# Seven products instead of eight for the last batch's first MLP product

## The chip, the cores and the metric

The kernel runs on one core of a Trainium2 chip. A core has five engines with their own instruction queues: TensorE (PE; matmuls, its weight loads are shown as PEld), VectorE (DVE), ScalarE (ACT), GpSimd (POOL) and SyncE (SP, which here only starts DMA transfers). Matmul results go to PSUM, which has eight banks of 512 floats in each of 128 partitions; everything else lives in SBUF. The metric is device time in microseconds of one execution, lower is better.

## The reference

There are 8 batches of 576 rows. First a linear attention over 8 heads of 64 columns, with position weights, then a low-rank mixing over the rows, then a two-layer MLP:

```python
r = np.maximum(x, 0.0)                         # x is q or k
phi = np.concatenate([r * cos, r * sin], -1)   # 128 features a head
kv = np.einsum('bhsf,bhsd->bhfd', k_p, v)
z = np.sum(k_p, axis=2)
x = np.einsum('bhsf,bhfd->bhsd', q_p, kv) / (np.einsum('bhsf,bhf->bhs', q_p, z) + 1e-6)
h = x.transpose(0, 2, 1) @ U @ V               # rank 32, over the rows
u = x + h.transpose(0, 2, 1)
out = u + np.maximum(u @ w_ch1, 0.0) @ w_ch2   # 512 -> 2048 -> 512
```

What matters here is `u @ w_ch1`, with relu, for one batch: 576 x 512 by 512 x 2048.

## The kernel before, in words

Of a batch's 576 rows, 512 are handled as four tiles of 128 rows ("main"), and the 64 rows left over ("tail") of two batches together make one more tile of 128. `uT[b]` holds the batch's u transposed: four blocks d of 128 channels, each with 4 x 128 rows. `w1_bf` and `w2_bf` hold the two weight matrices in 16 bits.

The work is laid out by hand as a list of slots. Each slot is one unit of matmuls; `todo` attaches other work (features, transposes, loads, sums) to slot numbers. Every engine takes its instructions in the order in which this list issues them; semaphores are set by the framework from what each instruction reads and writes. `starts[b]` is the slot at which batch b's first product begins. For each pair of batches there are, in this order: 16 slots of the even batch's first product, its 14 slots of the second product, 16 slots of the odd batch's first product, 4 slots of the pair's tail rows through the first layer, 14 slots of the odd batch's second product, 4 slots of the tail through the second layer.

The first product, `g1_main(b, j)`, makes 128 of the 2048 hidden columns in one slot: four matmuls (one for each channel block d) of 128 weights by 512 rows into one bank of the three called "g"; ScalarE applies the relu and writes 512 values to `hid[b]` (L550, L559). `g1_tail` does the same for the pair's tail rows, sixteen 128-column matmuls a slot, with one ScalarE relu (L570, L577).

The second product, `w_part(b, n)`, already uses a 2 x 2 block algorithm of the Strassen kind with seven products (Winograd's form): hidden columns are split into even and odd blocks of 128, rows into two halves of 256, and output columns into two halves. Seven steps of two slots each (`step, half = divmod(n, 2)`), 16 matmuls of 256 columns a step. The sums of weights, T, are made early in the kernel (`w2_form`); the sums of hidden blocks, S, are made by VectorE in halves (`hid_form(b, n, half)`, L696): form 1 is S1, form 2 is S2, form 3 is written over a block of `hid`, form 4 is S4. Half 0 covers the first four of the eight hidden blocks of a kind, half 1 the others; the first slot of a step reads half 0 alone. Results are joined by ScalarE (step 0's copy, `w_sum`), VectorE (L740) and GpSimd (three adds of `w_sum` and u, L740), and stored.

PSUM is used by tags: "g" has three banks, "T" one, "X" a pair of banks; two more are "oA" and "oB" in the beginning and, from slot 32 on (`pair_o`), one pair "O" for the attention's products. In SBUF, `qst`, `kst` and `vst` are the staging into which SP loads q, k and v of a batch, 10 KB a partition each. `k_p` and `q_p` hold the features made from them (8 KB each).

For the last batch, b = 7, the attention work is done when its first product begins; what runs beside it is only `hid_form` on VectorE.

Of the kernel before, what the change touches and what calls it, by code (L numbers as in the profile page):

```python
# [17 lines left out]
def kernel(  # L18
# [13 lines left out]
    B = 8  # L32
# [16 lines left out]
    def tail(b):  # L49
# [3 lines left out]
    const = ctx.enter_context(tc.tile_pool(name="const", bufs=1))  # L53
    pool = ctx.enter_context(tc.tile_pool(name="work", bufs=2))
    ps = ctx.enter_context(tc.tile_pool(name="ps", bufs=1, space=bass.MemoryType.PSUM))
    ps_rest = [ExitStack()]
    ps_o = ps_rest[0].enter_context(
        tc.tile_pool(name="ps_o", bufs=1, space=bass.MemoryType.PSUM)
    )

    ctx.enter_context(tc.manual_schedule())


    qst = const.tile([P, H, 5, D], FP32)
    kst = const.tile([P, H, 5, D], FP32)
    vst = const.tile([P, H, 5, D], FP32)

    def nines(src, b):
        return src[b].rearrange("h (m k) d -> m h (k d)", k=9)
# [40 lines left out]
    def cast(eng, o, i):  # L110
        if eng is nc.scalar:
            nc.scalar.activation(out=o, in_=i, func=AF.Copy, bias=0.0, scale=1.0)
        else:
            eng.tensor_copy(out=o, in_=i)  # L114
# [126 lines left out]
            G_.tensor_copy(out=V_qt[quarter(d), d, :], in_=V_tl[quarter(d), :])  # L241

    G3, T1, X1, OA, OB, O1 = ("g", 3), ("T", 1), ("X", 1), ("oA", 1), ("oB", 1), ("O", 1)
    turn = [0]

    def O2():
# [2 lines left out]

    def pair_o():  # L250
        ps_rest[0].close()
        ps_rest[0] = ctx.enter_context(
            tc.tile_pool(name="ps_O", bufs=1, space=bass.MemoryType.PSUM)
        )

    def bank(shape, dt, tag, bufs, name):
        if tag in ("oA", "oB"):
            return ps_o.tile(shape, dt, tag=tag, bufs=bufs, name=name)
        if tag == "O":
            t = ps_rest[0].tile([P, 2, 512], FP32, tag=tag, bufs=bufs, name=name)  # L260
            return t if len(shape) == 3 else t[:, 0, 0 : shape[1]]
        return ps.tile(shape, dt, tag=tag, bufs=bufs, name=name)

# [271 lines left out]

    hid, hid_tl = {}, {}

    g_open = {}

    def g1_main(b, j, half=False):  # L540
# [22 lines left out]
    def g1_tail(pr, jq):  # L563
        if pr not in hid_tl:
            hid_tl[pr] = pool.tile([P, NJ, P], BF16, tag="hid_tl", bufs=1, name="hid_tl")
        g_ps = ps.tile([P, 4, P], FP32, tag="g", bufs=3, name="gt_ps")
        for jj in range(4):
            j = jq * 4 + jj
            for d in range(4):
                nc.tensor.matmul(  # L570
                    out=g_ps[:, jj, :],
                    lhsT=w1_bf[:, d, j * P : j * P + P],
                    rhs=uT_tl[pr][:, d, :],
                    start=(d == 0),
                    stop=(d == 3),
                )
        nc.scalar.activation(  # L577
            out=hid_tl[pr][:, jq * 4 : jq * 4 + 4, :], in_=g_ps, func=AF.Relu,
            bias=0.0, scale=1.0,
        )  # L580
# [44 lines left out]
    def g2_tail(pr, part):  # L625
        last = pr == NPAIR - 1
        if part == 0 or last and part == 3:
            tag, bufs = T1 if part == 0 else O1
            o_ps[pr] = bank([P, DM], FP32, tag, bufs, "ot_ps")
        o = o_ps[pr]  # L630
        if last:
            cols = slice(0, 384) if part < 3 else slice(384, DM)
            js = (range(0, 5), range(5, 10), range(10, NJ), range(NJ))[part]
        else:
            cols, js = slice(0, DM), range(part * 4, part * 4 + 4)
        for j in js:
            nc.tensor.matmul(  # L637
                out=o[:, cols], lhsT=hid_tl[pr][:, j, :], rhs=w2_bf[:, j, cols],
                start=(j == 0), stop=(j == NJ - 1),
            )  # L640
        if js[-1] < NJ - 1:
            return
        if part == 2 or not last:
            o_sb[B + pr, 0] = pool.tile([P, DM], FP32, tag="o_tl", bufs=1, name="o_tl")
        o_s = o_sb[B + pr, 0]
        nc.vector.tensor_tensor(
            out=o_s[:, cols], in0=u_tl[pr][:, cols], in1=o[:, cols], op=ALU.add
        )
        for i in range(2):
            eng = store_eng(2 * pr) if part == 2 or not last else (nc.sync, nc.scalar)[i]  # L650
            eng.dma_start(
                out=out[2 * pr + i].rearrange("(m k) n -> m k n", k=9)[:, 4, cols],
                in_=o_s[i * TS : i * TS + TS, cols],
            )
# [21 lines left out]
    def hid_block(b, i, r, rows=slice(0, KB)):  # L676
        h = hid[b].rearrange("p (k i) t -> p k i t", i=2)
        return h[:, rows, i, r * 256 : r * 256 + 256]
# [30 lines left out]
    def w_part(b, n):  # L709
        step, half = divmod(n, 2)  # L710
        lhs, rhs, to = (
            (lambda: hid_block(b, 0, 0), w2_block(0, 0), 0),
            (lambda: s_forms[b, 2], T[1], 1),
            (lambda: s_forms[b, 1], T[0], 2),
            (lambda: s_forms[b, 3], T[2], 3),
            (lambda: hid_block(b, 1, 0), w2_block(1, 0), 0),
            (lambda: s_forms[b, 4], w2_block(1, 1), 2),
            (lambda: hid_block(b, 1, 1), T[3], 3),
        )[step]
        lhs = lhs()  # L720
        opens = step < 4
        if opens and half == 0:
            tag, bufs = T1 if to == 0 else G3
            w_ps[to] = bank([P, DM], FP32, tag, bufs, f"w_ps{to}")
        res = w_ps[to].rearrange("p (g n) -> p g n", g=2)
        for k_ in range(half * 4, half * 4 + 4):
            for g in range(2):
                nc.tensor.matmul(  # L728
                    out=res[:, g, :], lhsT=lhs[:, k_, g * P : g * P + P], rhs=rhs[:, k_, :],
                    start=(opens and k_ == 0 and g == 0),  # L730
                    stop=(k_ == KB - 1 and g == 1), skip_group_check=not opens,
                )
        for f in {0: (1, 2), 2: (3,), 4: (4,)}.get(n, ()):
            hid_form(b, f, 1)
        if half == 0:
            return
        lo, hi = slice(0, HD), slice(HD, DM)

        def add(eng, o, x, y):
            eng.tensor_tensor(out=o, in0=x, in1=y, op=ALU.add)  # L740

        def by_d(t):
            return t.rearrange("p c (d n) -> p d c n", n=P)

        def u(c0, h):
            return u_bf[b][:, 2 * h : 2 * h + 2, c0 : c0 + 2, :]

        if step == 0:
            w_sum[b] = pool.tile([P, 2, HD], FP32, tag="w_sum", bufs=1, name="w_sum")
            cast(A_, w_sum[b], res)  # L750
        elif step == 1:
            w = w_sum[b]
            o0, o1 = o_alloc(b, 0), o_alloc(b, 1)
            add(V_, w, w, res)
            add(G_, by_d(o1[:, :, hi]), by_d(w), u(2, 1))
            add(G_, by_d(o0[:, :, hi]), by_d(w), u(0, 1))
            add(G_, by_d(o1[:, :, lo]), by_d(w), u(2, 0))
        elif step == 2 or step == 3:
            o = o_sb[b, 1][:, :, hi]
            add(V_, o, o, res)  # L760
        elif step == 4:
            add(V_, by_d(o_sb[b, 0][:, :, lo]), u(0, 0), by_d(res))
        elif step == 5:
            o = o_sb[b, 0][:, :, hi]
            add(V_, o, o, res)
            store_w(b, 0, 0)
        else:
            o = o_sb[b, 1][:, :, lo]
            add(V_, o, o, res)
            store_w(b, 2, 1)  # L770
# [16 lines left out]
    def lay(units, in_second):  # L787
        slots.extend(units)
        second.extend([in_second] * len(units))

    def first_units(b):
        starts[b] = len(slots)
        lay([lambda j=j: g1_main(b, j) for j in range(NJ)], False)
        for i in range(4 * (b > 0)):
            beside.setdefault(starts[b] + (12 + 2 * i if b == 1 else 8 + i), []).append(
                lambda i=i: hid_form(b, (1, 2, 4, 3)[i], 0)
            )

    def second_units(b):
        lay([lambda n=n: w_part(b, n) for n in range(14)], True)  # L800
# [3 lines left out]
    def lay_all():  # L804
        for pr in range(NPAIR):
            e, o = 2 * pr, 2 * pr + 1
            first_units(e)
            if pr == 0:
                lay([lambda cc=cc, p=p: g2_part(cc, p) for p in range(4) for cc in range(4)], True)
            else:  # L810
                second_units(e)
            first_units(o)
            lay([lambda j=j, pr=pr: g1_tail(pr, j) for j in range(4)], False)
            second_units(o)
            lay([lambda p=p, pr=pr: g2_tail(pr, p) for p in range(4)], True)

# [239 lines left out]
    def gate(src):  # L1056
        nc.sync.dma_start(out=mark2, in_=src)
# [47 lines left out]
    def put(at, thunk):  # L1105
        todo.setdefault(at, []).append(thunk)

    put(15, lambda: gate(w2_bf[0:1, 4, 0:1]))
    put(70, release)
    put(72, release)  # L1110
    for n, t in enumerate(loads(2)):
# [38 lines left out]
```

## Time and profile before

| | us |
|---|---|
| median of 3 runs | 297.22 (296.43 to 297.79) |
| the profiled execution | 296.9 |
| its span, from the first to the last instruction | 295.1 |
| last batch: first matmul of the first product | 257.71 |
| first matmul of the tail rows | 271.52 |
| first matmul of the second product | 275.09 |
| first matmul of the tail's second layer | 287.32 |

The mean granted TensorE clock was 0.997. In a row of the timeline the first number is the start in us from the beginning of the span, the second the length of the group; matmuls are pipelined, so the time that one takes from the next is read from starts, not from the length of one. In a group's row the count stands behind x, then busy us and mean ns of one, then the idle time of its engine just before it and what ended that.

### The profile page before, as it was taken

The page shows a single profiled execution, that of the slowest core. Times are in us where ns is not written, and L with a number is a line of the kernel's source. Part 1 is how long each engine was busy: PE and PEld are TensorE (multiplying, and loading weights), DVE is VectorE, ACT ScalarE, POOL GpSimd, SP SyncE. Part 2 cuts the span into 40 slices and gives each one's busy share as a digit, 9 for nine tenths or more (in the row PEclk, how much of TensorE's full clock was granted, in tenths as well). Part 3 has the DMA queues.
Part 4 walks back from the last instruction along what each step waited for, and adds up shares of the span by engine and source line. Part 5 has one row for each costly group of instructions (what it writes and reads, how often), then busy time and mean ns, then how long its engine had stood idle before and what let it go on. Part 6 is the DMA issues. An engine that isn't in the chain of part 4 may idle for free.

```text
span 295.1 us, 7056 instructions
## 1 busy us (share of the span) xinstructions
PE 289.5 (98%) x2946; PEld 194.9 (66%) x2946; DVE 182.7 (62%) x358; ACT 159.1 (54%) x273; POOL 72.2 (24%) x113
## 2 busy tenths in 40 slices
PE   8999999999999999999999999999999999999994
PEld 6876455445987547855887547855887547845982
DVE  4979648897884578537744587537744586404331
ACT  2955641675692557646692557746692453066300
POOL 8430600140062304540051500540051101400040
PEclk9999999999999999999999999999999999999998
DMA  6999999999999995999679708995374104030004
GB/s 200 355 254 252 274 205 263 262 183 173 280 202 190 300 343 126 257 291 296 146 128 244 292 2 203 209 318 147 73 133 169 38 2 89 2 142 2 1 2 178
DMA packets 85283, 53.30 MB, mean 181 GB/s; under 512 B 54020, under 2 KB 82980, under 8 KB 85252
## 3 DMA queue, kind: packets, MB, share of 16 engines
q1 hardware_dynamic: 78804, 41.40, 58.1%
q0 software_dynamic: 6368, 11.43, 16.1%
q8 instruction: 23, 0.38, 0.5%
q14 instruction: 8, 0.07, 0.1%
q10 hardware_dynamic: 80, 0.03, 0.0%
HBM read 36.86 MB, written 9.44 MB: 157 GB/s over the span
## 4 chain that ended last, share of the span: by engine, by line
PE 98%; DVE 0%; ACT 0%; issue 0%
PE g_ps L550 38%; PE w_ps L728 29%; PE gt_ps L570 5%; PE o_ps L610 5%; PE ot_ps L637 5%; PE w_ps L200 3%; PE x_ps L412 3%; PE kv_ps L338 2%; PE a_ps L438 1%; PE va_ps L463 1%; PE kv_ps L319 1%; PE t_ps L355 1%; PE t_ps L367 1%; PE xh_ps L912 1%; PE va_ps L483 0%; PE xz L904 0%
## 5 line engine op out<-in xcount | busy, mean ns | idle before, releaser
L559 ACT ACTIVATE hid<-g_ps 128x512 bf16<-128x512 f32 x128 | 76.1, 597 | 85.5 <-PE g_ps L550 58.8
L550 PE MATMUL g_ps<-uT,w_bf 128*128 128x512 bf16 x512 | 120.6, 379 | 0.0
L550 PEld LDWEIGHTS <-w_bf 128*128 128x128 bf16 x512 | 46.3, 98 | 49.0 <-DMA w_bf<-in_moe_w_ch_dram 0.2
L740 POOL TENSOR_TENSOR o_sb<-w_sum,u_bf 128x512 f32<-128x512 f32 x21 | 26.4, 1280 | 125.9 <-DVE w_sum L740 125.9
L728 PEld LDWEIGHTS <-hid 128*128 128x128 bf16 x448 | 43.6, 98 | 5.6
L728 PEld LDWEIGHTS <-S 128*128 128x128 bf16 x336 | 32.6, 98 | 4.0
L740 DVE TENSOR_TENSOR o_sb<-o_sb,w_ps 128x512 f32<-128x512 f32 x28 | 19.2, 687 | 17.5 <-PE w_ps L728 11.0
L728 PE MATMUL w_ps<-w_bf,hid 128*128 128x256 bf16 x224 | 26.9, 273 | 0.0
L728 PE MATMUL w_ps<-T,hid 128*128 128x256 bf16 x224 | 26.7, 273 | 0.0
L728 PE MATMUL w_ps<-T,S 128*128 128x256 bf16 x224 | 25.9, 273 | 0.0
L472 DVE TENSOR_TENSOR u_bf<-x_bf,va_ps 128x1024 bf16<-128x1024 bf16 x16 | 19.3, 1216 | 7.2 <-PE va_ps L463 7.2
L114 POOL CAST v_ext<-vst 128x512 bf16<-128x512 f32 (+1 forms) x30 | 17.9, 635 | 12.0 <-DMA vst<-in_v_dram 11.6
L422 DVE TENSOR_TENSOR x_bf<-x_ps,rec 128x512 bf16<-128x512 f32 x28 | 19.4, 691 | 1.0
L696 DVE TENSOR_TENSOR S<-hid 128x1024 bf16<-128x1024 bf16 x14 | 9.6, 687 | 15.3 <-ACT hid L559 15.3
L402 DVE TENSOR_SCALAR rec<-x_ps 128x8 f32<-128x8 f32 (+1 forms) x35 | 5.7, 164 | 20.1 <-PE x_ps L412 20.0
L584 POOL DMA_DIRECT2D out_dram<-o_sb x12 | 7.6, 631 | 39.5 <-DVE o_sb L618 22.0
L282 ACT ACTIVATE k_p<-kst,sinw 128x512 bf16<-128x512 f32 x26 | 17.1, 712 | 0.3 <-DMA kst<-in_k_dram 0.3
L610 PE MATMUL o_ps<-w_bf,hid 128*128 128x512 bf16 x64 | 15.6, 379 | 0.0
L570 PEld LDWEIGHTS <-w_bf 128*128 128x128 bf16 x256 | 14.7, 98 | 0.9
L570 PE MATMUL gt_ps<-uT_tl,w_bf 128*128 128x128 bf16 x256 | 15.3, 219 | 0.0
L114 DVE CAST kv<-kv_ps 128x520 bf16<-128x520 f32 (+1 forms) x8 | 5.1, 632 | 16.3 <-PE kv_ps L338 11.8
L637 PE MATMUL ot_ps<-w_bf,hid_tl 128*128 128x512 bf16 (+2 forms) x80 | 15.0, 336 | 0.0
(154 smaller groups left out, 365.4 us busy)
## 6 DMA issues: line engine op xcount, KB each, us to landing
qst<-in_q_dram SPq DMA_DIRECT2D x14, 512.0 KB, 6.0
kst<-in_k_dram SPq DMA_DIRECT2D x14, 512.0 KB, 8.4
vst<-in_v_dram SPq DMA_DIRECT2D x12, 512.0 KB, 7.9
out_dram<-o_sb POOLq DMA_DIRECT2D x12, 512.0 KB, 6.8
w_bf<-in_moe_w_ch_dram POOLq DMA_DIRECT2D x8, 512.0 KB, 10.4
out_dram<-o_sb SPq DMA_DIRECT2D x4, 512.0 KB, 3.0
qst<-in_q_dram SPq DMA_DIRECT2D x2, 640.0 KB
kst<-in_k_dram SPq DMA_DIRECT2D x2, 640.0 KB, 10.9
```

The lines of the kernel that those rows point to most:

```text
L114: eng.tensor_copy(out=o, in_=i)
L282: nc.scalar.activation(out=o, in_=i, func=AF.Relu, bias=0.0, scale=w)
L422: nc.vector.tensor_tensor(out=x_of(b, c, rows).rearrange("p (g i d) -> p g i d", g=2, d=D), in0=view[:, :, :, 0:D], in1=rec[rows].unsqueez ...
L472: nc.vector.tensor_tensor(out=u_bf[b][:, d0 : d0 + 2], in0=x_bf[b].rearrange("p c (d n) -> p d c n", n=P)[:, d0 : d0 + 2], in1=va_ps[b, d0 ...
L550: nc.tensor.matmul(out=g_ps.rearrange("p (c t) -> p c t", c=4), lhsT=w1_bf[:, d, j * P : j * P + P], rhs=uT[b][:, d, :, :], start=(d == 0) ...
L559: nc.scalar.activation(out=hid[b][:, j, :], in_=g_ps, func=AF.Relu, bias=0.0, scale=1.0)
L570: nc.tensor.matmul(out=g_ps[:, jj, :], lhsT=w1_bf[:, d, j * P : j * P + P], rhs=uT_tl[pr][:, d, :], start=(d == 0), stop=(d == 3),)
L610: nc.tensor.matmul(out=o, lhsT=hid[0][:, j, cc * P : cc * P + P], rhs=w2_bf[:, j, :], start=(j == 0), stop=(j == NJ - 1),)
L637: nc.tensor.matmul(out=o[:, cols], lhsT=hid_tl[pr][:, j, :], rhs=w2_bf[:, j, cols], start=(j == 0), stop=(j == NJ - 1),)
L696: V_.tensor_tensor(out=o, in0=a, in1=b_, op=op)
L728: nc.tensor.matmul(out=res[:, g, :], lhsT=lhs[:, k_, g * P : g * P + P], rhs=rhs[:, k_, :], start=(opens and k_ == 0 and g == 0), stop=(k_ ...
L740: eng.tensor_tensor(out=o, in0=x, in1=y, op=ALU.add)
```

## The change

For b = 7 the first product is done in 2 x 2 blocks too: the 512 channels in two halves (dh), the 512 rows in two halves (r), and the 2048 hidden columns in even and odd blocks of 128 (i). The hidden columns come in four groups m = a, b, c, d of two even and two odd blocks. Each group has seven products, called parts, each of four matmuls of 256 columns (two blocks by two channel blocks), so 4 x 7 x 4 matmuls.

Parts 1, 6, 5 and 3 of a group accumulate on one bank, and ScalarE reads it after each of them: a copy of 1 (`pw`), of 1+6 (`pw`), of 1+6+5 (`py`), and the relu of all four, which is one of the group's four hidden blocks. Part 2 goes to the first bank of X; VectorE adds it to the copy of 1 and applies the relu in place. Part 7 goes to a bank "g"; VectorE adds the copy of 1+6+5, then the relu. Part 4 continues on 7's bank; VectorE adds the copy of 1+6, then the relu.

The order of parts and of the four tail slots ("t") is written out in `LAST`, with six of the eight halves of the S sums ("f10" is form 1, half 0); the two others come in the second product.

The sums of weights (`sa`, eight VectorE additions of 1024 16-bit elements) and of `uT` (`tb`, four of 512) are made ahead: the first four beside the tail slots of batch 5, the next four beside slots 1, 3, 5 and 7 of batch 6's second product, and the four of `uT` beside its slots 8 to 11. They lie where `vst`, `qst` and `kst` were, which is why the staging is now taken from a pool that can hand the space on; `pw` and `py` lie where `k_p` and `q_p` were. At slot 8 of batch 6's second product the pair "O" is given back and two single banks "oA" and "oB" are taken in its place. The tail's last quarter uses "oA" instead of "O".

```diff
+    w1_k = w1_bf.rearrange("p d (k i n) -> p d k i n", i=2, n=P)
...
+    def w1_form(n, hf, tag):
...
+        a, b_, op = (
+            (w1_block(1, 0, ks), w1_block(1, 1, ks), ALU.add),
+            (t[:, 0], w1_block(0, 0, ks), ALU.subtract),
+            (w1_block(0, 0, ks), w1_block(1, 0, ks), ALU.subtract),
+            (w1_block(0, 1, ks), t[:, 1], ALU.subtract),
+        )[n]
+        V_.tensor_tensor(out=t[:, n], in0=a, in1=b_, op=op)
...
+    def g1_part(b, m, part):
...
+        lhs, rhs = {
+            1: lambda: (w1_block(0, 0, ks), uT_block(b, 0, 0)),
+            2: lambda: (w1_block(0, 1, ks), uT_block(b, 1, 0)),
+            3: lambda: (s_of(3), uT_block(b, 1, 1)),
+            4: lambda: (w1_block(1, 1, ks), tb[b][:, 3]),
+            5: lambda: (s_of(0), tb[b][:, 0]),
+            6: lambda: (s_of(1), tb[b][:, 1]),
+            7: lambda: (s_of(2), tb[b][:, 2]),
+        }[part]()
+        if part == 1:
+            g_al[b, m] = bank([P, DM], FP32, *(OA, OB, T1)[m % 3], "al_ps")
+        elif part in (2, 7):
+            g_be[b, m, part] = bank([P, DM], FP32, *(X1S if part == 2 else G3), "be_ps")
+        t = g_al[b, m] if part in (1, 3, 5, 6) else g_be[b, m, 2 if part == 2 else 7]
+        opens = part in (1, 2, 7)
...
+        for k_ in range(2):
+            for d in range(2):
+                nc.tensor.matmul(
+                    out=res[:, k_, :], lhsT=lhs[:, d, k_, :], rhs=rhs[:, d, :],
...
+        def relu(o):
+            V_.tensor_scalar(out=o, in0=o, scalar1=0.0, scalar2=None, op0=ALU.max)
+
+        def add(o, x):
+            V_.tensor_tensor(out=o, in0=x, in1=res, op=ALU.add)
+
+        if part == 1:
+            cast(A_, p_, res)
+        elif part == 6:
+            cast(A_, w_, res)
+        elif part == 5:
+            cast(A_, y_, res)
+        elif part == 3:
+            nc.scalar.activation(
+                out=block(0, 1), in_=res, func=AF.Relu, bias=0.0, scale=1.0
+            )
+        elif part == 2:
+            add(block(0, 0), p_)
+            relu(block(0, 0))
+        elif part == 7:
+            add(block(1, 1), y_)
+            relu(block(1, 1))
+        else:
+            add(block(1, 0), w_)
+            relu(block(1, 0))
...
-        for f in {0: (1, 2), 2: (3,), 4: (4,)}.get(n, ()):
+        for f in ({0: (4,), 2: (3,)} if b == B - 1 else {0: (1, 2), 2: (3,), 4: (4,)}).get(n, ()):
...
+    LAST = (
+        "1a 2a", "t", "6a 1b", "t", "5a 7a", "2b 6b", "3a 1c", "4a 5b", "7b 2c", "6c 3b",
+        "1d 4b", "5c 7c", "2d 6d", "3c f10 4c", "5d 7d f20", "t", "3d f11 f21", "t", "4d f40 f30",
+    )
...
+    s6 = starts[B - 2]
+    for n in range(4):
+        put(starts[B - 3] + 16 + n, lambda n=n: w1_form(n, 0, "vst"))
+        put(s6 + 17 + 2 * n, lambda n=n: w1_form(n, 1, "qst"))
+        put(s6 + 24 + n, lambda n=n: uT_form(B - 1, n, "kst"))
+    put(s6 + 24, split_o)
```

More of the change, by code (lines that the diff above doesn't have):

```diff
@@ L55 @@
     ps = ctx.enter_context(tc.tile_pool(name="ps", bufs=1, space=bass.MemoryType.PSUM))
-    ps_rest = [ExitStack()]
-    ps_o = ps_rest[0].enter_context(
-        tc.tile_pool(name="ps_o", bufs=1, space=bass.MemoryType.PSUM)
+    ps_rest = [ctx.enter_context(ExitStack())]
+    ps_rest.append(
+        ps_rest[0].enter_context(
+            tc.tile_pool(name="ps_o", bufs=1, space=bass.MemoryType.PSUM)
+        )
     )
     ctx.enter_context(tc.manual_schedule())
-    qst = const.tile([P, H, 5, D], FP32)
-    kst = const.tile([P, H, 5, D], FP32)
-    vst = const.tile([P, H, 5, D], FP32)
+    qst, kst, vst = (
+        pool.tile([P, H, 5, D], FP32, tag=n, bufs=1, name=n) for n in ("qst", "kst", "vst")
+    )
     def nines(src, b):
@@ L243 @@
     G3, T1, X1, OA, OB, O1 = ("g", 3), ("T", 1), ("X", 1), ("oA", 1), ("oB", 1), ("O", 1)
+    X1S = ("x", 1)
     turn = [0]
@@ L251, in pair_o, with split_o @@
         ps_rest[0].close()
-        ps_rest[0] = ctx.enter_context(
-            tc.tile_pool(name="ps_O", bufs=1, space=bass.MemoryType.PSUM)
+        ps_rest.append(
+            ps_rest[0].enter_context(
+                tc.tile_pool(name="ps_O", bufs=1, space=bass.MemoryType.PSUM)
+            )
+        )
+    def split_o():
+        ps_rest[0].close()
+        ps_rest[1] = ps_rest[0].enter_context(
+            tc.tile_pool(name="ps_s", bufs=1, space=bass.MemoryType.PSUM)
         )
     def bank(shape, dt, tag, bufs, name):
+        if tag == "x":
+            return ps.tile([P, 2, 512], FP32, tag="X", bufs=1, name=name)[:, 0, 0 : shape[1]]
         if tag in ("oA", "oB"):
-            return ps_o.tile(shape, dt, tag=tag, bufs=bufs, name=name)
+            return ps_rest[1].tile(shape, dt, tag=tag, bufs=bufs, name=name)
         if tag == "O":
-            t = ps_rest[0].tile([P, 2, 512], FP32, tag=tag, bufs=bufs, name=name)
+            t = ps_rest[2].tile([P, 2, 512], FP32, tag=tag, bufs=bufs, name=name)
             return t if len(shape) == 3 else t[:, 0, 0 : shape[1]]
@@ L536, with w1_block @@
     hid, hid_tl = {}, {}
+    w1_k = w1_bf.rearrange("p d (k i n) -> p d k i n", i=2, n=P)
+    sa, tb, pw, g_al, g_be = {}, {}, {}, {}, {}
+    def w1_block(i, dh, ks):
+        return w1_k[:, 2 * dh : 2 * dh + 2, ks, i, :]
+    def w1_form(n, hf, tag):
+        if hf not in sa:
+            sa[hf] = pool.tile([P, 4, 2, 4, P], BF16, tag=tag, bufs=1, name=f"sa{hf}")
+        t = sa[hf]
+        ks = slice(4 * hf, 4 * hf + 4)
+        a, b_, op = (
[5 more added lines that the diff above has]
+        V_.tensor_tensor(out=t[:, n], in0=a, in1=b_, op=op)
@@ new lines, in uT_block, with uT_form @@
+    def uT_block(b, dh, r):
+        return uT[b][:, 2 * dh : 2 * dh + 2, 2 * r : 2 * r + 2, :].rearrange(
+            "p d c t -> p d (c t)"
+        )
+    def uT_form(b, n, tag):
+        if b not in tb:
+            tb[b] = pool.tile([P, 4, 2, 256], BF16, tag=tag, bufs=1, name="tb")
+        t = tb[b]
+        a, b_ = (
+            (uT_block(b, 0, 1), uT_block(b, 0, 0)),
+            (uT_block(b, 1, 1), t[:, 0]),
+            (uT_block(b, 1, 1), uT_block(b, 0, 1)),
+            (uT_block(b, 1, 0), t[:, 1]),
+        )[n]
+        V_.tensor_tensor(out=t[:, n], in0=a, in1=b_, op=ALU.subtract)
@@ new lines, in g1_part, with s_of, block @@
+    def g1_part(b, m, part):
+        if b not in hid:
+            hid[b] = pool.tile([P, NJ, 512], BF16, tag="hid", bufs=1, name="hid")
+        if b not in pw:
+            pw[b] = (
+                pool.tile([P, 4, 512], FP32, tag="k_p", bufs=1, name="pw"),
+                pool.tile([P, 2, 512], FP32, tag="q_p", bufs=1, name="py"),
+            )
+        ks = slice(2 * m, 2 * m + 2)
+        hf, k0 = divmod(2 * m, 4)
+        def s_of(n):
+            return sa[hf][:, n, :, k0 : k0 + 2, :]
+        lhs, rhs = {
[13 more added lines that the diff above has]
+        opens = part in (1, 2, 7)
+        res = t.rearrange("p (k n) -> p k n", k=2)
+        for k_ in range(2):
+            for d in range(2):
+                nc.tensor.matmul(
+                    out=res[:, k_, :], lhsT=lhs[:, d, k_, :], rhs=rhs[:, d, :],
+                    start=(opens and k_ == 0 and d == 0), stop=(k_ == 1 and d == 1),
+                    skip_group_check=not opens,
+                )
+        e = m % 2
+        p_, w_, y_ = (
+            t_.rearrange("p (k n) -> p k n", k=2)
+            for t_ in (pw[b][0][:, 2 * e], pw[b][0][:, 2 * e + 1], pw[b][1][:, e])
+        )
+        def block(i, r):
+            return hid_block(b, i, r, ks)
+        def relu(o):
[11 more added lines that the diff above has]
+                out=block(0, 1), in_=res, func=AF.Relu, bias=0.0, scale=1.0
+            )
+        elif part == 2:
[7 more added lines that the diff above has]
+            relu(block(1, 0))
@@ L627, in g2_tail @@
         if part == 0 or last and part == 3:
-            tag, bufs = T1 if part == 0 else O1
+            tag, bufs = T1 if part == 0 else OA
             o_ps[pr] = bank([P, DM], FP32, tag, bufs, "ot_ps")
@@ L793, in first_units @@
         lay([lambda j=j: g1_main(b, j) for j in range(NJ)], False)
-        for i in range(4 * (b > 0)):
+        for i in range(4 * (0 < b)):
             beside.setdefault(starts[b] + (12 + 2 * i if b == 1 else 8 + i), []).append(
@@ L797, in first_units, with last_units, unit, go @@
             )
+    LAST = (
+        "1a 2a", "t", "6a 1b", "t", "5a 7a", "2b 6b", "3a 1c", "4a 5b", "7b 2c", "6c 3b",
+        "1d 4b", "5c 7c", "2d 6d", "3c f10 4c", "5d 7d f20", "t", "3d f11 f21", "t", "4d f40 f30",
+    )
+    def last_units(b, pr):
+        starts[b] = len(slots)
+        t = iter(range(4))
+        def unit(names):
+            tails = [next(t) for n in names if n == "t"]
+            def go():
+                for n in names:
+                    if n == "t":
+                        g1_tail(pr, tails[0])
+                    elif n[0] == "f":
+                        hid_form(b, int(n[1]), int(n[2]))
+                    else:
+                        g1_part(b, "abcd".index(n[1]), int(n[0]))
+            return go
+        lay([unit(n.split()) for n in LAST], False)
     def second_units(b):
@@ L811, in lay_all @@
                 second_units(e)
-            first_units(o)
-            lay([lambda j=j, pr=pr: g1_tail(pr, j) for j in range(4)], False)
+            if o == B - 1:
+                last_units(o, pr)
+            else:
+                first_units(o)
+                lay([lambda j=j, pr=pr: g1_tail(pr, j) for j in range(4)], False)
             second_units(o)
```

## The prediction

> **What bounds the kernel now.** I read the busy shares first, then the chain of waits in order of time, then the last batch instruction by instruction.
>
> ```profile
> PE 289.5 (98%) x2946; PEld 194.9 (66%) x2946; DVE 182.7 (62%) x358; ACT 159.1 (54%) x273; POOL 72.2 (24%) x113
> ...
> 249.90 7.97 PE w_ps L728 x73
> 257.87 13.81 PE g_ps L550 x64
> 271.68 3.57 PE gt_ps L570 x64
> 275.26 12.23 PE w_ps L728 x112
> 287.48 3.51 PE ot_ps L637 x32
> ```
>
> TensorE is the chain from end to end. Whatever takes matmul time out of the stretch 257.7 to 275.1 us (the last batch's first product and its tail rows) moves the end by as much, provided nobody makes TensorE wait instead. The same stretch by engine (length, then PE, PEld, DVE, ACT, POOL busy, then the granted clock), with the one behind it and the end:
>
> ```profile
> 257.70:275.10 17.40, 17.40 (x131) 9.81 (x129) 5.35 (x8) 11.35 (x19) 0.00 (x0) 1.00 0.15 61
> 275.10:287.30 12.20, 12.20 (x115) 10.94 (x113) 4.04 (x6) 1.20 (x2) 3.72 (x3) 1.00 0.01 2
> 287.30:295.10 7.80, 3.68 (x34) 2.45 (x32) 1.53 (x3) 0.00 (x0) 0.00 (x0) 0.90 0.47 168
> ```
>
> VectorE has 12 us free in it, ScalarE 6 us. These lines of the timeline and of the groups by shape give the prices:
>
> ```profile
> 257.71 13.98 PE L550 MATMUL g_ps<-uT,w_bf 128*128 128x512 bf16 x64
> ...
> 271.52 3.74 PE L570 MATMUL gt_ps<-uT_tl,w_bf 128*128 128x128 bf16 x64
> ...
> 275.09 1.91 PE L728 MATMUL w_ps<-w_bf,hid 128*128 128x256 bf16 x16
> ...
> 276.84 3.66 PE L728 MATMUL w_ps<-T,S 128*128 128x256 bf16 x32
> 277.10 0.60 ACT L112 ACTIVATE w_sum<-w_ps 128x512 f32<-128x512 f32 x1 [1.21 <-PE w_ps L728]
> ```
> ```profile
> L422 DVE TENSOR_TENSOR x_bf<-x_ps,rec 128x512 bf16<-128x512 f32 x28 | 19.4, 691 | 1.0
> L284 DVE TENSOR_SCALAR k_p<-kst,cosw 128x512 bf16<-128x512 f32 x23 | 10.1, 478 | 0.0
> L696 DVE TENSOR_TENSOR S<-hid 128x1024 bf16<-128x1024 bf16 x14 | 9.6, 687 | 15.3 <-ACT hid L559 15.3
> L402 DVE TENSOR_SCALAR rec<-x_ps 128x8 f32<-128x8 f32 x28 | 4.6, 164 | 13.8 <-PE x_ps L412 13.7
> ```
>
> From start to start, a 512-column matmul takes (271.52-257.71)/64 = 0.2158 us, a 256-column one (276.84-275.09)/16 = 0.109, a 128-column one (275.09-271.52)/64 = 0.0558. ScalarE starts 0.26 us after the last matmul's slot ends (277.10 against 276.84) and takes 0.60.
>
> **The matmuls.** Removed: 64 of 512 columns, 13.81 us. Added: 4 groups x 7 products x 4 matmuls = 112 of 256 columns, 12.21 us. Gain on TensorE: 1.60 us, 0.54% of the time; that is all the change can win. The 64 tail matmuls only move in between, as four blocks of 0.89 us; a product takes 0.436 us. The tail's transposed rows, now wanted at 258.6 instead of 271.3, were sent off by SP at 246.16.
>
> **Turn-round of an accumulator.** Products 1, 6, 5, 3 of a group go onto one bank; each waits until ScalarE has copied the one before: 0.26 + 0.60 + the step back to TensorE, R. TensorE hardly ever waits in this trace. At the start it loaded weights 0.07 us after ScalarE ended, and a matmul came 0.31 us after VectorE's normalization ended (18.03 to 18.34 us). So R is 0.05 to 0.31; I take 0.15, between, since other work may have caused part of the 0.31. The loop is then 1.01 us. Of the 12 such loops 11 have at least three products (1.31 us) or a tail block and one product (1.33) between them: no wait. 6d to 5d has two products, 0.87: a wait of 0.14 (0.04 to 0.30). ScalarE itself: 20 casts of 0.60, as before 20.
>
> **VectorE, the term that decides.** Products 2, 7, 4 of each group are joined by it: an add of 512 floats, 0.69 (the normalization's row has the same shape), and a relu in place, r, which waits for the add (0.04 more); the next add starts some 0.08 before the relu ends, as back-to-back rows do. A pair costs 0.65 + r. No row shows a relu from 16-bit to 16-bit. Bounds: 0.16 (the 8-element row, all overhead) and 0.48 (the same operation on 32-bit input). In the additions 1024 16-bit elements take the 0.69 us of 512 32-bit ones, so I halve the streaming part: 0.164 + (0.478-0.164)/2 = 0.32, nearest to neither end but supported by a row of this engine. The Trainium skill, "VectorE: DVE Perf Modes", section "The perf-mode tier table", gives such an operation four elements a cycle, and with the fixed 150 cycles that the page measured I estimate 0.29 us; the sum would be that of 0.32. By the float row as it stands the sum differs, and that is rival B.
>
> A group takes TensorE 7 x 0.436 = 3.05 us and VectorE 3 x (0.65 + r): 2.91 at 0.32, and 3.05 at r = 0.367. So VectorE keeps up, narrowly, from 262.6 on, with the tail blocks as reserve. Closest is 4c, which adds onto 7c's bank. 7c's join needs the copy of 5c, issued until 267.78: 267.78 + 0.26 + 0.60 + 0.03 = 268.67; it ends at 269.36, with R 269.51, and 4c is due at 269.52: a wait of 0 to 0.15.
>
> Behind the joins stand the eight sums S (0.61 from start to start, 0.73 where one reads the one before). From 268.67 VectorE runs without a gap: 7c and 2d to 270.61, half a sum to 271.22, 4c and 7d to 273.16, three halves, the last of them S2's second half, which ends at 275.2; its weights are wanted at 276.2. Then 4d and four more halves: the last ends at 278.6, wanted at 279.7, and w_sum's add starts at 278.5, 0.4 us earlier than now. GpSimd's three adds follow (1.28 each), and step 2's add ends at 281.3 where TensorE wants that bank at 282.3. No wait.
>
> **Sums made ahead.** Eight of weights at 0.69 and four of 512 16-bit elements at about 0.43 (0.164 + half of 0.533): 7.2 us of VectorE, no DMA, no semaphore that is late. Four stand before batch 5's S sums: the second half of S2 ends at 213.99 instead of 211.43, its product loads at 214.6; the two features behind it end at 215.9, SP sends their transposes at 216.09; step 1's add was due at 215.86. The covers are 0.6 us and 0.2 us; the add of step 1 has none and is 0 late. Of batch 6's, step 2's add is not delayed (it waits for GpSimd until 251.58), step 3's by 0.13 us with its bank wanted 2.5 us later. The transposed rows that the last four read left SP at 242.92, and the sums run from 254.0. Up to batch 5's tail the instructions and waits of all queues are the same; the staging's addresses move only. I take zero; the bounds are 0 and +0.6 (the S2 half that much later than worked out); a gain is excluded, as nothing is taken away there.
>
> **Sum.** -1.60 + 0.14 (5d) + 0.05 (4c) = -1.4 us. The profiled execution took 296.9 (span 295.1, 1.8 around it), so 295.5 there; it lies 0.3 under the median 297.22, so I expect 295.8 (span 293.7). Half a per cent, 1.5 us, is about what a measurement of this kernel tells from no change: the forecast stands just inside that bound.
>
> **Rivals.** A is the forecast, -1.55 to -1.1.
>
> B, VectorE becomes the bound: the relu costs 0.40 to 0.48 as the float row has it. Some nine pairs in a row then run behind, each 0.01 us over 0.367 costs 0.09: at 0.43, 0.5 us lost (296.3); at 0.48, 1.0 lost (296.8). Against it: the 16-bit additions' rate.
>
> C, turn-rounds are longer: R at 0.45 or more. Then 5d waits 0.4, 4c 0.3, and the loops of 1.31 us start to wait; -1.0 to -0.6, 296.2 to 296.6. For it: 0.31 is seen once. Against: 0.07 is seen too.
>
> D, slower: the in-place relu runs at one element a cycle, as PSUM reads do (0.69 for 512). r = 0.70 is 0.33 over the limit, times nine 3.0 us: +1.5, 298.7. It decides from r = 0.69 up. Only an unseen shape speaks for it, and every SBUF row against it.
>
> E, the waits lower the clock. The granted clock is 0.90 where TensorE runs dry at the end, 1.00 elsewhere; the stage's 15.8 us at 0.90 would be 1.75 longer: 297.5, no change. Against it: between 8 and 20 us TensorE had several short waits and kept 1.00. The Trainium skill, "TensorE: Matmul & The Clock Gate", section "A second HAM failure mode: psum-queue depth-cycling", says that micro-idles between groups that cycle through PSUM banks make the clock swing between half and full; no stretch of this trace bears that out.
>
> **How the numbers follow.** A 0.63, B 0.18, C 0.08, D 0.05, E 0.03, the rest 0.03. With half of A's runs falling past 1.5 us once a median's scatter of some 0.4 us is added, faster is 0.34; slower is D and some of the rest, 0.08; same 0.58. The range goes from the full 1.6 with scatter (295.1) to the end of B and C (297.1); A alone 295.4 to 296.2.
>
> **What will show it.** Right: 112 matmuls at 0.109 and no idle over 0.3 us on TensorE between 257.7 and 273.7; the w products start at 273.6; the relu at 0.3; joins of 7c start at 268.7. Wrong: TensorE idle at 4c, the third tail block and 4d, released by VectorE (B, D); idle at many products released by ScalarE (C); a clock under 1.00 (E); a later start than 257.7, if the sums made ahead did reach the chain.

## The result and the profile after

The changed kernel takes 295.97 us (median of 6 runs, 295.49 to 296.19) against 297.75 (median of 6, 296.43 to 299.05) of the kernel before, measured beside it: ratio 0.9939, 95% interval 0.9911 to 0.9967. That is 0.61% less. The interval leaves out no change at all, but it has in it the half per cent that the prediction took as the least change that such a measurement can tell, so by that bound the result counts as "same". A second measurement, among the experiments below, gave 0.9951 (0.9930 to 0.9973), which reads alike. The forecast was 295.8. The ratios are of executions in the chip's fast state alone and can differ by up to 0.1% from the quotient of the medians given here.

The profiled execution took 296.14 us with a span of 294.4 and a mean granted clock of 0.996. First the busy shares of the changed kernel, then the end of its chain of waits:

```profile
PE 287.9 (98%) x2994; PEld 199.0 (68%) x2994; DVE 201.3 (68%) x394; ACT 158.0 (54%) x273; POOL 75.0 (25%) x113
```
```profile
246.47 12.23 PE w_ps L849 x112
258.70 0.44 PE al_ps L619 x4
...
274.08 0.44 PE be_ps L619 x4
274.52 12.22 PE w_ps L849 x112
286.74 3.51 PE ot_ps L758 x32
```

TensorE has 1.6 us less work, VectorE 18.6 more, and the chain is TensorE's alone from 246 us on, as it was before: no piece of VectorE or ScalarE stands in it until the last addition of the output. A window of the changed kernel shows the new product (length, then PE, PEld, DVE, ACT, POOL busy, the granted clock, DMA share, GB/s):

```profile
258.53:274.36 15.83, 15.83 (x179) 14.54 (x177) 12.07 (x26) 10.61 (x20) 0.00 (x0) 1.00 0.17 68
```

And the timeline of the changed kernel, with one join from beginning to end. A part is named by its number and its group: the rows from 269.50 on are 7c's addition, ScalarE's copy of 6d, 7c's relu, and the matmuls of 4c and of 5d.

```profile
258.53 0.60 PE L619 MATMUL al_ps<-uT,w_bf 128*128 128x256 bf16 x4
...
269.50 0.69 DVE L637 TENSOR_TENSOR hid<-py,be_ps 128x512 bf16<-128x512 f32 x1
270.18 0.60 ACT L114 ACTIVATE pw<-al_ps 128x512 f32<-128x512 f32 x1 [0.70 <-PE al_ps L619]
270.23 0.29 DVE L634 TENSOR_SCALAR hid<-hid 128x512 bf16<-128x512 bf16 x1
270.36 0.60 PE L619 MATMUL be_ps<-tb,w_bf 128*128 128x256 bf16 x4
270.82 0.60 PE L619 MATMUL al_ps<-tb,sa 128*128 128x256 bf16 x4
...
274.36 1.91 PE L849 MATMUL w_ps<-w_bf,hid 128*128 128x256 bf16 x16
275.13 0.69 DVE L817 TENSOR_TENSOR S<-S,hid 128x1024 bf16<-128x1024 bf16 x1
...
286.58 3.66 PE L758 MATMUL ot_ps<-w_bf,hid_tl 128*128 128x384 bf16 x32
```

The stage, from the first matmul of the last batch's first product to the first of its second product, is the measure for everything below. Before, it went from 257.71 to 275.09, 17.38 us; now from 258.53 to 274.36, 15.83 us. That is a gain of 1.55, in a stage whose matmuls alone need 12.21 + 3.57 = 15.78: TensorE waits no more than 0.05 us in all of it. The second product takes 286.58 - 274.36 = 12.22, as before (287.32 - 275.09 = 12.23), and what follows is alike.

The span, however, is only 0.7 us shorter than in the profile before, because the stage began 0.82 later. The trace shows where that arose: TensorE waited longer for weights from memory in batch 0, first at its first product (26.63 before, 27.03 here), then at its second (39.02 and 39.84), and from there to 257.7 us the distance stayed.

```profile
27.03 1.04 PE L671 MATMUL g_ps<-uT,w_bf 128*128 128x512 bf16 x4 [0.28 <-DMA w_bf<-in_moe_w_ch_dram]
...
39.84 1.02 PE L731 MATMUL o_ps<-w_bf,hid 128*128 128x512 bf16 x4 [0.28 <-DMA w_bf<-in_moe_w_ch_dram]
```

So two things were to be tested: whether the change itself makes the start later (through its new addresses or its sums ahead), and whether the reasons given for the stage (a relu of about 0.3 us, VectorE just under TensorE, accumulators turned round in time) are the ones that held.

### The profile page after: what moved, and what is told of

The parts are those of the page before. It is cut to its first block, busy times and chain, and to the rows that moved or that the text cites. A ratio compares the mean times of both kernels' runs of the same rounds, so it can differ in the third digit from the quotient of the medians.

```text
span 294.4 us, 7205 instructions
## 1 busy us (share of the span) xinstructions
PE 287.9 (98%) x2994; PEld 199.0 (68%) x2994; DVE 201.3 (68%) x394; ACT 158.0 (54%) x273; POOL 75.0 (25%) x113
## 4 chain that ended last, share of the span: by engine, by line
PE 88%; DMA 9%; DVE 1%; issue 0%; ACT 0%; POOL 0%; ACTq 0%; POOLq 0%; DVEq 0%
PE w_ps L849 29%; PE g_ps L671 29%; PE gt_ps L691 5%; PE o_ps L731 5%; DMA kst<-in_k_dram 5%; PE ot_ps L758 5%; PE x_ps L425 3%; DMA w_bf<-in_moe_w_ch_dram 3%; PE kv_ps L351 2%; PE al_ps L619 2%; DMA qst<-in_q_dram 2%; PE be_ps L619 2%; PE a_ps L451 1%; PE t_ps L380 1%; PE va_ps L476 1%; PE w_ps L202 1%
## 5 line engine op out<-in xcount | busy, mean ns | idle before, releaser
L671 PE MATMUL g_ps<-uT,w_bf 128*128 128x512 bf16 x448 | 106.7, 379 | 0.3 <-DMA w_bf<-in_moe_w_ch_dram 0.3
L680 ACT ACTIVATE hid<-g_ps 128x512 bf16<-128x512 f32 x112 | 66.5, 597 | 71.4 <-PE g_ps L671 44.7
L671 PEld LDWEIGHTS <-w_bf 128*128 128x128 bf16 x448 | 40.0, 98 | 42.2 <-DMA w_bf<-in_moe_w_ch_dram 1.0
L861 POOL TENSOR_TENSOR o_sb<-w_sum,u_bf 128x512 f32<-128x512 f32 x21 | 27.0, 1308 | 121.7 <-DVE w_sum L861 121.7
L116 POOL CAST v_ext<-vst 128x512 bf16<-128x512 f32 (+1 forms) x30 | 19.7, 692 | 14.0 <-DMA vst<-in_v_dram 13.6
L116 DVE CAST kv<-kv_ps 128x520 bf16<-128x520 f32 (+1 forms) x8 | 5.1, 632 | 16.8 <-PE kv_ps L351 11.8
L691 PEld LDWEIGHTS <-w_bf 128*128 128x128 bf16 x256 | 14.9, 98 | 0.8
L425 PEld LDWEIGHTS <-q_pT 128*128 128x128 bf16 x224 | 10.8, 98 | 5.9
```

Source lines behind the costliest of these rows:

```text
L425: nc.tensor.matmul(out=acc[:, g, i * E : i * E + E], lhsT=qT_of(b, c, h), rhs=kv_sb[b][:, h, :], start=True, stop=True,)
L671: nc.tensor.matmul(out=g_ps.rearrange("p (c t) -> p c t", c=4), lhsT=w1_bf[:, d, j * P : j * P + P], rhs=uT[b][:, d, :, :], start=(d == 0) ...
L680: nc.scalar.activation(out=hid[b][:, j, :], in_=g_ps, func=AF.Relu, bias=0.0, scale=1.0)
L691: nc.tensor.matmul(out=g_ps[:, jj, :], lhsT=w1_bf[:, d, j * P : j * P + P], rhs=uT_tl[pr][:, d, :], start=(d == 0), stop=(d == 3),)
```

## The experiments

### The kernel before, once more

The kernel before, unchanged, beside the next three.

> The kernel before against itself, for the scatter of time and of the early weight loads: ratio 1 within 0.3%; the last batch's first matmul, 257.71 us in the first profile, moves by some tenths up to 1 us if the weights' arrival is what scatters, by less than 0.1 if it is not.

Measured: 297.29 us, ratio 0.9994 (0.9978 to 1.0010). Its own profile, from the timeline:

```profile
257.27 1.36 PE L728 MATMUL w_ps<-T,hid 128*128 128x256 bf16 x11
258.47 3.83 PE L550 MATMUL g_ps<-uT,w_bf 128*128 128x512 bf16 x16
```

Its last batch begins at 258.47, 0.76 later than in the first profile of the same kernel; 0.56 of that is there by 42 us and 0.2 came at about 115 us, in batch 2 (the last section shows where). The start of the stage moves by this much with nothing changed. Its length does not: the second product begins at 275.85, so it is 17.38 again.

### The staging from a pool, alone

```diff
-    qst = const.tile([P, H, 5, D], FP32)
-    kst = const.tile([P, H, 5, D], FP32)
-    vst = const.tile([P, H, 5, D], FP32)
+    qst, kst, vst = (
+        pool.tile([P, H, 5, D], FP32, tag=n, bufs=1, name=n) for n in ("qst", "kst", "vst")
+    )
```

> The kernel before, with only the staging tiles taken from the pool; nothing uses their space afterwards. My theory: the last batch's first product started 0.82 us later in the changed kernel's profile (258.53 against 257.71), all of it before 40 us, where TensorE waited for weights from HBM, and that is the scatter of one execution, not the change. Then this kernel's time is that of the kernel before within 0.3%, and its last batch starts anywhere from 257.5 to 258.8 us. Rival: the new addresses of the staging make the early loads later; then this kernel is 0.4 to 0.8 us slower, and its first weights are waited for as in the changed kernel (first product of batch 0 at 27.0 instead of 26.6, its second product at 39.8 instead of 39.0).

Measured: 297.25 us, ratio 1.0007 (0.9978 to 1.0035); the last batch begins at 257.71, to the hundredth where it began before. The new addresses cost nothing.

### The sums made ahead, alone

The changed kernel with its twelve sums, but with the first product, the tail slots and the banks of the last batch as before.

```diff
...
-            if o == B - 1:
-                last_units(o, pr)
-            else:
-                first_units(o)
-                lay([lambda j=j, pr=pr: g1_tail(pr, j) for j in range(4)], False)
+            first_units(o)
+            lay([lambda j=j, pr=pr: g1_tail(pr, j) for j in range(4)], False)
...
-    put(s6 + 24, split_o)
```

> The changed kernel with the twelve sums made ahead (7.2 us of VectorE), but the last batch's first product as before; the sums are made and not used. My theory: they are hidden, so the time is that of the kernel before, 0 to 0.1% off, and TensorE has no wait between 208 and 257 us. Rival: the four sums in front of batch 5's S2 or the eight in batch 6 reach the chain and cost 0.2 to 0.6 us.

Measured: 297.42 us, ratio 0.9995 (0.9977 to 1.0012). The stage began 0.32 later than in the profile before, but 0.30 of that arose in batch 2, at about 115 us, and the first of the sums runs at about 209. From 118 us on the distance stays, past all twelve sums, and the stage is 17.39 long. The sums are free.

### The change, once more

> The changed kernel once more, on the chip of the others. Theory: 0.5% faster than the kernel before (-1.5 us), the stretch from the last batch's first matmul to its second product 15.8 us again (17.4 before), and another start of that stretch than 258.53. Rival: the late start is the change's, 258.5 again, and the gain in time half of what the stretch gives.

Measured: 295.92 us (295.19 to 297.39) against 297.31, ratio 0.9951 (0.9930 to 0.9973). The stage ran from 258.87 to 274.69, 15.82 us. Its late start, 1.16 against the first profile before, was 0.79 by 39 us, and the rest came in batch 2, at about 116 us. In the profiles of these four experiments the stage thus began between 257.71 and 258.87, each time for reasons before 118 us. Its length repeats to 0.01 us: 17.38 and 17.39 with the old product, 15.82 and 15.83 with the new one.

### The relu twice

```diff
         def relu(o):
-            V_.tensor_scalar(out=o, in0=o, scalar1=0.0, scalar2=None, op0=ALU.max)
+            for _ in range(2):
+                V_.tensor_scalar(out=o, in0=o, scalar1=0.0, scalar2=None, op0=ALU.max)
```

> The changed kernel, each of the twelve in-place relus of VectorE done twice (the second changes nothing). Theory: VectorE keeps up with little to spare; a group of seven products takes TensorE 3.05 us and VectorE 3 x (0.65 + r), the relu was 0.294 in the changed kernel's profile, so 2.83; twice (0.29 + 0.04 + 0.29 - the overlap) makes it 3.6 a group, 0.55 over. TensorE then waits at 4b, 4c, the third tail block and 4d, about 2 us in all; the stretch from the last batch's first matmul to its second product grows from 15.8 to 18.0 us, and the whole gain is lost: +0.5 us against the kernel before. Rival: VectorE has slack (it was 75% busy in that stretch), the products lie far enough apart, and the stretch grows by less than 0.5.

Measured: 298.19 us, ratio 1.0016 (0.9995 to 1.0038): the whole gain is gone. Its timeline, two additions on VectorE and then the three longest waits of TensorE:

```profile
266.38 0.68 DVE L638 TENSOR_TENSOR hid<-pw,be_ps 128x512 bf16<-128x512 f32 x1
267.09 0.62 DVE L635 TENSOR_SCALAR hid<-hid 128x512 bf16<-128x512 bf16 x2
267.63 0.68 DVE L638 TENSOR_TENSOR hid<-py,be_ps 128x512 bf16<-128x512 f32 x1
...
272.11 0.60 PE L619 MATMUL be_ps<-tb,w_bf 128*128 128x256 bf16 x4 [0.97 <-DVE hid L638]
...
275.21 1.05 PE L692 MATMUL gt_ps<-uT_tl,w_bf 128*128 128x128 bf16 x16 [0.30 <-DVE hid L638]
...
276.47 0.60 PE L619 MATMUL be_ps<-tb,w_bf 128*128 128x256 bf16 x4 [0.20 <-DVE hid L638]
```

A join now takes 1.25 us from start to start, a group 3.75 against TensorE's 3.05, and the debt shows in the starts of the blocks: 4b comes 0.13 after its turn, 4c 1.13, the fourth tail block 0.46 (the third had been expected) and 4d 0.37, together 2.09 (a start's distance from the block ahead, less that block's 0.436 or 0.89). The stage is 17.88 long, 2.05 over the change's. By the prediction's rule of nine joins in a row, 9 x (1.25 - 1.017) is 2.10, with 1.017 for a third of a group on TensorE. This is a milder form of what rival D would have looked like: 0.62 for the two relus and not 0.70.

### The join in 32 bits

The addition writes the 32-bit copy in place, and the relu reads 32 bits and writes 16.

```diff
-        def add(o, x):
-            V_.tensor_tensor(out=o, in0=x, in1=res, op=ALU.add)
+        def join(o, x):
+            V_.tensor_tensor(out=x, in0=x, in1=res, op=ALU.add)
+            V_.tensor_scalar(out=o, in0=x, scalar1=0.0, scalar2=None, op0=ALU.max)
```

> The changed kernel with the joins' sum kept as 32-bit floats (added in place into the copy) and the relu reading those floats. My rival B as a kernel. Theory: the relu takes 0.43 to 0.48 us instead of 0.294; beyond 0.367 each 0.01 us costs 0.09, so the stretch grows by 0.5 to 1.0 us, to 16.3 to 16.8, and the gain against the kernel before is 0.5 to 1.0 us instead of 1.5. Rival: no loss, since the tail blocks give VectorE reserve enough.

Measured: 296.2 us, ratio 0.9950 (0.9912 to 0.9987), which the times alone don't tell from the change. The stage does: 257.17 to 273.32, 16.15 us, 0.32 more than the change's and below the 16.3 to 16.8 expected. The starts show where: 4c comes 0.11 after its turn, the fourth tail block 0.08 and 4d 0.17. From the timeline, one join and the next:

```profile
263.09 0.68 DVE L634 TENSOR_TENSOR pw<-pw,be_ps 128x512 f32<-128x512 f32 x1
263.80 0.43 DVE L635 TENSOR_SCALAR hid<-pw 128x512 bf16<-128x512 f32 x1
264.14 0.68 DVE L634 TENSOR_TENSOR pw<-pw,be_ps 128x512 f32<-128x512 f32 x1
```

The relu takes 0.427, the join 1.05 to 1.06 from start to start, so a join is 0.63 + r, and not the 0.65 + r of the prediction. With that the threshold is r = 1.017 - 0.63 = 0.387, and nine joins lose 9 x (0.427 - 0.387) = 0.36; the stage lost 0.32. Rival B is a true mechanism; its price was put too high (0.5 us at 0.43), because its threshold was put 0.02 too low.

### Without VectorE's relus

```diff
         def relu(o):
-            V_.tensor_scalar(out=o, in0=o, scalar1=0.0, scalar2=None, op0=ALU.max)
+            pass
```

> The changed kernel without the twelve relus of VectorE (three of four hidden blocks of the last batch then lack the relu, so the output differs there). Theory: in the changed kernel TensorE is the bound of the stretch, which is 15.8 us with or without them; time as the changed kernel's, 0.1 us less at most. Rival: VectorE still costs something (the joins were within 0.2 us of being late at 4c), and the stretch gets 0.2 to 0.5 us shorter.

Measured: 295.83 us, ratio 0.9946 (0.9906 to 0.9985); the stage 258.09 to 273.94, 15.85 us. Twelve instructions less on VectorE shorten nothing. In the changed kernel the relus cost zero, and TensorE alone is the bound.

### The tail blocks at the end

The four tail blocks behind the seven-product groups and not between them.

```diff
     LAST = (
-        "1a 2a", "t", "6a 1b", "t", "5a 7a", "2b 6b", "3a 1c", "4a 5b", "7b 2c", "6c 3b",
-        "1d 4b", "5c 7c", "2d 6d", "3c f10 4c", "5d 7d f20", "t", "3d f11 f21", "t", "4d f40 f30",
+        "1a 2a", "6a 1b", "5a 7a", "2b 6b", "3a 1c", "4a 5b", "7b 2c", "6c 3b",
+        "1d 4b", "5c 7c", "2d 6d", "3c f10 4c", "5d 7d f20", "3d f11 f21", "4d f40 f30",
+        "t", "t", "t", "t",
     )
```

> The changed kernel with the four tail blocks behind the products, as they stood before the change, the order otherwise the same. Theory: between 1a and 6a, and between 5d and 3d, only one product (0.44 us) is left for a turn-round of 0.25 + 0.60 + 0.04 = 0.89 us: 0.45 to 0.5 of waiting at each; and VectorE, without the blocks' 3.6 us beside it, is late at 4c, 3d or 4d by 1.0 more. The stretch is 17.3 to 17.9 us, no gain against the kernel before (-0.1 to +0.5). Rival: the order does not matter since TensorE's work is the same, and the stretch stays under 16.3.

Measured: 298.03 us, ratio 1.0011 (0.9989 to 1.0033), the gain gone again; the stage 258.86 to 277.04, 18.18 us, above the range expected. Its timeline, a turn-round of an accumulator first, then all of TensorE's long waits:

```profile
259.55 0.60 ACT L114 ACTIVATE pw<-al_ps 128x512 f32<-128x512 f32 x1 [10.30 <-PE al_ps L619]
260.20 0.60 PE L619 MATMUL al_ps<-tb,sa 128*128 128x256 bf16 x4 [0.30 <-ACT pw L114]
...
261.48 0.60 PE L619 MATMUL al_ps<-tb,sa 128*128 128x256 bf16 x4 [0.25 <-ACT pw L114]
...
271.85 0.60 PE L619 MATMUL al_ps<-uT,sa 128*128 128x256 bf16 x4 [0.59 <-ACT py L114]
...
273.03 0.60 PE L619 MATMUL be_ps<-tb,w_bf 128*128 128x256 bf16 x4 [0.58 <-DVE hid L637]
```

Each is where a tail block stood before: 6a and 5a wait 0.46 and 0.41 (the number in brackets is a little less, since the last matmul's modelled end is later than its slot's), 3d and 4d wait 0.75 each, together 2.37. The wait at 5a had not been counted in the expectation: with one product between 6a and 5a the loop is 0.85 and the cover 0.44. At 3d 0.28 is open: ScalarE's copy of 5d began 0.53 after that product's last slot where the copies of 1a and 6a began 0.25 and 0.20 after theirs, and no run here says why. So the order of `LAST` is worth more than the change itself: 112 cheaper matmuls in a worse order gain nothing.

## Why the prediction was right

**Matmuls, -1.60.** Measured as -1.55 over the stage, with the 0.05 us of waits in it. 112 matmuls came at 0.109 each. This is the one term that moves the time, and it was read from starts of rows of the kernel before.

**Turn-round, R = 0.15, the 5d wait +0.14.** The copy of 6d ended at 270.18 + 0.60 = 270.78 and 5d started at 270.82, so R is 0.04 here; in the last experiment the loop ran from the end of 1a's slots at 259.30 over 0.25 and 0.60 to 6a at 260.20, 0.90 in all, with R = 0.05. Against its turn at 270.80, 5d waited 0.02. The lower bound, 0.05, was the right value. The 0.31 after the normalization, which pulled the estimate up, was not all this step: in the same trace the weight load for that matmul began at 18.08, 0.05 after the normalization's end, and the rest lay between the load and the matmul. Rival C falls with it.

**4c, +0.05.** 7c's addition ended at 269.50 + 0.69 = 270.19 and 4c began at 270.36, in its turn. No wait. Of the two waits of the sum, 0.19, some 0.02 came; this is most of why the stage gained 1.55 and not 1.4.

**The relu, r = 0.32.** By groups of the changed kernel:

```profile
L634 DVE TENSOR_SCALAR hid<-hid 128x512 bf16<-128x512 bf16 x12 | 3.5, 294 | 0.4
```

It is 0.294. The Trainium skill, "VectorE: DVE Perf Modes", section "The perf-mode tier table", with the 150 cycles, had given an estimate of 0.29, and the trace agrees; the row-based 0.32 was high because it halved the streaming part of 0.314, where with the same fixed 0.164 only 0.13 is left for it. A join took 267.55 to 268.48 = 0.93, a group on VectorE 2.79, under TensorE's 3.05 by 0.26 and not by 0.14. That VectorE "keeps up, narrowly" was right: one more relu a join, and it doesn't.

**The sums S behind the joins.** Counted from the later start of 0.82, each event came where it was put or a little before: 7c's join at 269.50 (268.67 + 0.82), S2's second half ready at 275.13 + 0.69 = 275.82 (275.2 + 0.82 = 276.0), wanted at 276.98, after the first 24 matmuls of the second product. No wait, as forecast.

**The sums ahead, 0.** Right, shown by the run with the sums alone. The last four of `uT` ran from 255.98, 1.2 us later than put even with the later start counted (254.0 + 0.82), for a reason told at the end; the first product that needs one of them, 6a, came at 260.30, and the last sum was done at 258.60.

**The clock, rival E.** It stayed at 1.00 in the stage, and also in the two experiments in which blocks started up to 1.13 and 0.75 us after their turn. The warning of the Trainium skill ("TensorE: Matmul & The Clock Gate", section "A second HAM failure mode: psum-queue depth-cycling") is not borne out by any stage of these runs.

**What the sum left out.** "A later start than 257.7" had been named as the sign that the sums ahead reach the chain. It came, and it was not that: the start differed by 0.76 us between two profiles of the kernel before, and lay between 257.17 and 259.02 in the profiles of kernels with the new product. A start compared across two single profiles could not bear that reading. The forecast stood on the median, so the scatter cancelled there: the two measured differences of medians, 1.78 and 1.39, lie on both sides of the stage's 1.55. That 295.8 came within 0.2 us of the 295.97 is in part luck: the kernel before, put at 297.22 from three runs, came to 297.75 in six, and the larger gain made up for it. And 1.55 of 297.5 is 0.52%, at the half per cent itself, so the time alone cannot decide well between "faster" and "same"; the stage can.

## What to carry to other kernels

Less matmul time on a saturated TensorE pays in full only if every accumulator that is read between products has its turn-round covered: here 0.25 + 0.60 + 0.05 = 0.90 us, a little over two products of 0.436, or one and a filler block, and the filler's place in the order was worth more than the arithmetic saved. Cost the engine that joins the results per group against TensorE's time per group; the excess of a join, times the joins in a row (here about nine), is what the stage loses. Here that gave 0.36 for 0.32 with a relu of 0.43 us, and 2.10 for 2.05 with two of 0.29. For a change below 1% measure the stage from its own first matmul to the next stage's first, and not by when it begins or ends in one profile.

## What the hardware showed that was not expected

VectorE and GpSimd slowed each other. In batch 6 the changed kernel runs 16-bit additions with both inputs in SBUF on VectorE while GpSimd does its three additions of the second product; the timeline of those two engines:

```profile
250.68 0.69 DVE L568 TENSOR_TENSOR sa<-sa,w_bf 128x1024 bf16<-128x1024 bf16 x1
250.84 4.67 POOL L861 TENSOR_TENSOR o_sb<-w_sum,u_bf 128x512 f32<-128x512 f32 x3 [18.77 <-DVE w_sum L861]
251.28 1.65 DVE L817 TENSOR_TENSOR S<-hid,S 128x1024 bf16<-128x1024 bf16 x1
252.85 0.68 DVE L861 TENSOR_TENSOR o_sb<-o_sb,w_ps 128x512 f32<-128x512 f32 x1
253.45 1.05 DVE L568 TENSOR_TENSOR sa<-w_bf 128x1024 bf16<-128x1024 bf16 x1
...
255.02 1.04 DVE L568 TENSOR_TENSOR sa<-w_bf,sa 128x1024 bf16<-128x1024 bf16 x1
```

The same stretch of the kernel before:

```profile
249.85 0.68 DVE L696 TENSOR_TENSOR S<-hid,S 128x1024 bf16<-128x1024 bf16 x1
250.02 3.76 POOL L740 TENSOR_TENSOR o_sb<-w_sum,u_bf 128x512 f32<-128x512 f32 x3 [18.76 <-DVE w_sum L740]
251.58 0.69 DVE L740 TENSOR_TENSOR o_sb<-o_sb,w_ps 128x512 f32<-128x512 f32 x1 [1.05 <-POOL o_sb L740]
```

Three VectorE instructions that take 0.69 elsewhere took 1.65, 1.05 and 1.04, and GpSimd's three took 4.67 where they had 3.76; the profile of the repeated change and of the sums alone have the same numbers to 0.01. The additions that read PSUM kept their 0.68. The Trainium skill, "SBUF — State Buffer", section "Who interferes with whom", says that a VectorE instruction with two SBUF inputs contends with a GpSimd instruction that reads SBUF; the rows agree, though whether one blocks the other wholly or they share, they don't tell. In batch 6 it cost nothing, since TensorE waited for neither; in the stage of the new product GpSimd has no work at all.

In batch 2, which the change leaves as it was, it does cost. There two of VectorE's sums S for the second product run beside GpSimd's four casts of v. The timeline of the repeated change:

```profile
114.15 3.40 POOL L116 CAST v_ext<-vst 128x512 bf16<-128x512 f32 x4 [2.08 <-DMA vst<-in_v_dram]
114.22 1.08 DVE L817 TENSOR_TENSOR S<-hid 128x1024 bf16<-128x1024 bf16 x1 [0.64 <-ACT hid L680]
115.34 0.98 DVE L817 TENSOR_TENSOR S<-S,hid 128x1024 bf16<-128x1024 bf16 x1
...
116.38 2.79 PE L849 MATMUL w_ps<-T,S 128*128 128x256 bf16 x24 [0.20 <-DVE S L817]
```

In six of the ten profiles the first of the two sums began 0.05 to 0.26 us after one of the casts. It then took 0.90 to 1.11 instead of 0.69, the second, which TensorE waits for, came later by as much, and the matmuls behind it were 0.2 to 0.4 us late. In the four others the first began before a cast or near a cast's end, took 0.69, and TensorE did not wait. These are the steps at about 115 us that moved the start of the stage, in the kernel before as in the changed one.
